# Attention and token-mixing kernel: head and token transposes moved from TensorE to transposing DMAs, with a new order of the mix steps and more products of zeros at the start

## The chip, the cores and the metric

The kernel runs on one core of one Trainium2 chip. The metric is the device time of one execution in microseconds (us). A profile's span is about 1.9 us shorter than the time of the same run. All runs compared here are of the state "fast"; two timed runs that were marked slow (346.0 us in e8, 346.2 us in e12) are left out of ratios and medians. Ratios are computed as the mean time of one kernel's fast runs over that of the other's of the same rounds, so they are not quite the ratio of the medians that are quoted.

## The reference

Block-sparse attention (4 batches, 8 heads, 768 tokens, 64 per head), then a residual MLP that first mixes tokens, then channels:

```python
scores = scale * np.matmul(q, k.transpose(0, 1, 3, 2))
mask = (abs(blk_i - blk_j) <= 1) | first and last blocks | sampled blocks
attn = softmax(np.where(mask, scores, -1e9))
x = (attn @ v), heads side by side            # (4, 768, 512)
a1 = alpha1 * x + beta1
u = x + lam * np.einsum('ts,bsd->btd', w_tok, a1)
a2 = alpha2 * u + beta2
out = u + lam * (np.maximum(a2 @ w_ch1, 0.0) @ w_ch2)
```

## The kernel before

A head pair is worked off in nine **units**. A unit is 1,024 score columns in PSUM and one exponential on ScalarE; there are 16 pairs, so 144 units. The products of attention and values follow two units later. When a pair is done, its **token mix** is queued, and between the units a filler emits first-layer (ch1) and second-layer (ch2) products.

The scores need q and k with the head dimension on partitions, so each head is transposed. Rows 64 to 87 of the transposed tiles hold the mask as 24 more contraction rows (block indicators in `kx`, mask values in `qx`), loaded once:

```python
def prepare(b, n):
    q2, k2, v2 = loaded.pop((b, n))
    rel = wk.tile([P, 2, NT, 2 * D], BF, name="rel", tag="rel", bufs=2)
    for i, src in enumerate((q2, k2)):
        nc.vector.tensor_copy(out=rel[:, :, :, i * D : (i + 1) * D], in_=...)
    yield
    for a in range(2):
        flat = transposes(rel, a)          # six TensorE transposes into an "mm" tile
        h = (2 * n + a) % NQB
        nc.vector.tensor_copy(out=qx[h][0:D, :], in_=flat[0:D, :])
        nc.vector.tensor_copy(out=kx[h][0:D, :], in_=flat[D:P, :])
        yield
# pair_mix(b, n), its end: the mixed tokens transposed for the first layer
    up = mm_tile([P, NT, P], BF)
    for t in range(NT):
        nc.tensor.transpose(up[:, t, :], ub[:, t, :], identb[:])
    nc.vector.tensor_copy(out=uTs[b][:, n, :], in_=up[:]...)
# mix_next(i): when a queued mix may start its VectorE part
    if m["dry"] and m["due"] <= i and (i >= len(units) or 1 <= i % NU <= 4):
```

The `mm` tiles (two PSUM buffers) serve these transposes, the token mix and the first layer alike. Cuts are marked with "..." or left out between functions.

The softmax here doesn't subtract the row's maximum and nothing guards it: scores larger than these inputs give would overflow.

Of the kernel before, what the change touches and what calls it, by code (L numbers as in the profile page):

```python
# [13 lines left out]
BF = mybir.dt.bfloat16  # L14
I32 = mybir.dt.int32
# [21 lines left out]
NS = NPAIR * NU  # L37
LAG = 2
SCALE = 1.0 / 8.0
EXPB = -0.35667494  # L40
# [23 lines left out]
def kernel(  # L64
# [33 lines left out]
    ).astype(np.float32)  # L98
    kbi_np = np.tile(np.arange(NBLK, dtype=np.float32), (NBLK, 1))

    tab_np = np.concatenate([mstat_np, kbi_np], axis=1)

    ident_dr = nc.inline_tensor(ident_np, name="ident_c")
    ind_dr = nc.inline_tensor(ind_np, name="ind_c")
    tab_dr = nc.inline_tensor(tab_np, name="tab_c")

# [18 lines left out]
    identb = pp.tile([P, P], BF, name="identb", tag="identb")  # L125
    qx = [pp.tile([P, S], BF, name=f"qx{i}", tag=f"qx{i}") for i in range(NQB)]
    kx = [pp.tile([P, S], BF, name=f"kx{i}", tag=f"kx{i}") for i in range(NQB)]
    vext = [
# [23 lines left out]
    q2f = wk.tile([P, 2, NT * D], FP, name="q2f", tag="hts", bufs=2)  # L152
    k2f = wk.tile([P, 2, NT * D], FP, name="k2f", tag="hts", bufs=2)
    nc.sync.dma_start(q2f[:, 0, :], pair_ap(q, 0, 0)[:, 0, :])
    nc.scalar.dma_start(k2f[:, 0, :], pair_ap(k, 0, 0)[:, 0, :])
    nc.sync.dma_start(sampi[MB, :], sampled_blocks.bitcast(I32))
    nc.scalar.dma_start(tab[MB, :], tab_dr.ap())
    nc.sync.dma_start(identb[:], ident_dr.ap())
    nc.scalar.dma_start(kx[0][MB, :], ind_dr.ap())
    nc.sync.dma_start(q2f[:, 1, :], pair_ap(q, 0, 0)[:, 1, :])  # L160
    nc.sync.dma_start(k2f[:, 1, :], pair_ap(k, 0, 0)[:, 1, :])
    for i in range(1, NQB):
        nc.sync.dma_start(kx[i][MB, :], ind_dr.ap())

    def load_pair(b, n):
# [20 lines left out]

    keep_warm(7, 512)
    for t in vext:
        nc.vector.memset(t[:, :, :, D:VW], 1.0)


# [18 lines left out]

    rel0 = wk.tile([P, 2, NT, 2 * D], BF, name="rel", tag="rel", bufs=2)

# [8 lines left out]

    def transposes(rel, a, slots=range(NT)):
        tps = mm_tile([P, NT, P], BF)
        for o in slots:
            nc.tensor.transpose(tps[:, o, :], rel[:, a, o, :], identb[:])  # L225
        return tps[:].rearrange("p o c -> p (o c)")

    first_cast(0)
    bq_ps = ps.tile([P, UN], FP, name="sps", tag="sps", bufs=2)
    for w in (0, 1):  # L230
        nc.tensor.matmul(
            bq_ps[0:NBLK, w * 512 : w * 512 + HS],
            mbb[MB, :],
            kx[0][MB, ts(w, HS)],
            start=True,
            stop=True,
        )
    flatA = transposes(rel0, 0, range(0, 3))
    flatB = transposes(rel0, 0, range(3, 6))
    nc.vector.tensor_copy(out=qx[0][MB, 0:HS], in_=bq_ps[0:NBLK, 0:HS])  # L240
    nc.scalar.copy(out=qx[0][MB, HS:S], in_=bq_ps[0:NBLK, 512 : 512 + HS])
    nc.vector.tensor_copy(out=kx[0][0:D, 0:HS], in_=flatA[D:P, 0:HS])
# [4 lines left out]
    for j in range(1, NQB):  # L247
        nc.sync.dma_start(qx[j][MB, :], qx[0][MB, :])


    def prepare(b, n):

        q2, k2, v2 = loaded.pop((b, n))
        vs[(b, n)] = v2
        rel = wk.tile([P, 2, NT, 2 * D], BF, name="rel", tag="rel", bufs=2)
        for i, src in enumerate((q2, k2)):
            nc.vector.tensor_copy(  # L257
                out=rel[:, :, :, i * D : (i + 1) * D],
                in_=src[:].rearrange("p h (o d) -> p h o d", o=NT),
            )  # L260
        yield
        for a in range(2):
            flat = transposes(rel, a)
            h = (2 * n + a) % NQB
            nc.vector.tensor_copy(out=qx[h][0:D, :], in_=flat[0:D, :])  # L265
            nc.vector.tensor_copy(out=kx[h][0:D, :], in_=flat[D:P, :])  # L266
            yield

    vs = {}
# [69 lines left out]
    def pair_mix(b, n):  # L339
# [19 lines left out]
        for g in range(NT // m):  # L359
            tp = mm_tile([P, m, P])  # L360
            for j in range(m):
                for s in range(NT):
                    nc.tensor.matmul(  # L363
                        tp[:, j, :],
                        wtokT[:, s, ts(m * g + j, P)],
                        a1p[:, s, :],
                        start=(s == 0),
                        stop=(s == NT - 1),
                    )
                if m == 2 and j == 0:  # L370
                    yield NT * T_MM128, 1, True
            gs = slice(m * g, m * g + m)
            sl = x_sb[:, s0 + m * g : s0 + m * g + m, cs]
            nc.vector.tensor_tensor(out=sl, in0=sl, in1=tp[:], op=ALU.add)  # L374
            nc.vector.tensor_tensor(  # L375
                out=ub[:, gs, :], in0=sl, in1=bc(a2_bc, m), op=ALU.mult
            )
            wait = 1 if g < NT // m - 1 else 5 if last else 2
            yield (1 if m == 2 else m) * NT * T_MM128, wait
        up = mm_tile([P, NT, P], BF)  # L380
        for t in range(NT):
# [9 lines left out]
    def ch1_group(k, f, tail):  # L391
# [8 lines left out]
        for dk in range(4):  # L400
# [6 lines left out]
            )  # L407
        if f % 2 == 0:
            nc.scalar.activation(  # L409
                hts[k][:, f, :], hp[:, 0:HS], AF.Relu, bias=b1t[:, f : f + 1], scale=1.0  # L410
            )
        else:
            nc.vector.tensor_scalar(  # L413
                out=hts[k][:, f, :],
                in0=hp[:, 0:HS],
                scalar1=b1t[:, f : f + 1],
                scalar2=0.0,
                op0=ALU.add,
                op1=ALU.max,
            )  # L420
# [36 lines left out]

    def setup_ch():
        nc.vector.tensor_copy(out=be2b[:], in_=be2T[:])
        for g in range(4):  # L460
            bp = mm_tile([P, 4])
            for f in range(4):
                for dk in range(4):
                    nc.tensor.matmul(
                        bp[:, f : f + 1],
                        w1b[:, dk, ts(4 * g + f, P)],
                        be2b[:, dk : dk + 1],
                        start=(dk == 0),
                        stop=(dk == 3),
                    )  # L470
            nc.vector.tensor_copy(out=b1t[:, ts(g, 4)], in_=bp[:])
            yield 16 * 30, 1

# [16 lines left out]
    for g in range(3):  # L490
        nc.gpsimd.dma_start(
            wtk[:, 2 * g : 2 * g + 2, :], wtk_ap[:, 2 * g : 2 * g + 2, :]
        )
    for t, src in ((lam_bc, moe_lam), (a1_bc, moe_alpha1), (b1_bc, moe_beta1)):
        nc.gpsimd.dma_start(t[:], src.unsqueeze(0).to_broadcast([P, DM]))
    loaded[(0, 2)] = load_pair(0, 2)
    loaded[(0, 3)] = load_pair(0, 3)
# [18 lines left out]
    def ch_next(tail=False):  # L516
# [4 lines left out]
        can1 = (  # L521
            g1 < NF1 and k1 // 2 < st["mixed"] and (k1 < 2 or g2 >= 12 * (k1 - 1))
        )
        can2 = g2 < NF2 and (
            g1 > 16 * (k2 + 1) or g1 == 16 * (k2 + 1) and st["at"] < st["i"]
# [18 lines left out]
    def mix_next(i):  # L544

        for m in mixq[:3]:
            if m["dry"] and m["due"] <= i and (i >= len(units) or 1 <= i % NU <= 4):
                m["due"] = i + next(m["gen"])[1]
# [27 lines left out]
    for i in range(len(units) + LAG):  # L576
# [3 lines left out]
        if i < len(units):  # L580
            b, n, u = units[i]
            pi = b * NPAIR + n
            emit_qk(b, n, u)
            if i == 2:

                vs[(0, 0)] = loaded.pop((0, 0))[0]
                put_v(0, 0)
                first_cast(1)
                flat = transposes(rel0, 1)
                nc.vector.tensor_copy(out=qx[1][0:D, :], in_=flat[0:D, :])  # L590
                nc.vector.tensor_copy(out=kx[1][0:D, :], in_=flat[D:P, :])
            if u == 0:
                if 0 < pi and pi + 3 < len(pairs):
# [4 lines left out]
            if i in (20, 22, 24, 26):  # L598
# [6 lines left out]
                )  # L605
            if u == 5 and pi + 1 < len(pairs):
                prep = prepare(*pairs[pi + 1])
            if prep is not None and u in (5, 7, 0):
                next(prep, None)
            if u == 8 and pi + 1 < len(pairs):  # L610
                put_v(*pairs[pi + 1])
            if i == 8:
                mix_add(None, setup_tok(), i)
            if i == 11:
                nc.vector.tensor_mul(out=a1_bc[:], in0=a1_bc[:], in1=lam_bc[:])
                nc.vector.tensor_mul(out=b1_bc[:], in0=b1_bc[:], in1=lam_bc[:])
            if i == NS:
                mix_add(None, setup_ch(), i)
            if NS + 10 <= i < NS + 26 and i % 2 == 0:
# [17 lines left out]
        if i >= LAG:  # L637
# [5 lines left out]
            while pv_done < lim:  # L643
# [3 lines left out]
                if r == GP - 1:  # L647
                    mix_add(pairs[j], pair_mix(*pairs[j]), max(i, 12))
        if mixq and not (i < NS and i % NU in (7, 0)):
            spent += mix_next(i)  # L650
# [42 lines left out]
```

## Time and profile before

| | before |
|---|---|
| median of 3 runs | 353.97 us (352.94 to 357.5) |
| span of the profiled run | 355.1 us |
| granted clock, mean over the span | 0.979 |
| exponentials number 1, 37, 55 and 144 start at | 8.9, 50.1, 89.5, 286.1 us |

In the views PE is TensorE, PEld its weight loads, DVE VectorE, ACT ScalarE, POOL GpSimd and SPq the queue of SyncE, from which the transposing DMAs are issued in order. The granted clock is the share of full speed that TensorE's clock was given.

The four exponentials cut the span into batch 0 (units 0 to 35), a stretch in which the later work is being filled in (units 36 to 53), and a regular rest. The views that carry the argument are printed in the prediction. The profiled run of before is one of its slower ones: its device time was 357.0 us. A difference of spans against it therefore overstates the gain by some 2 us, and I use medians for totals.

### The profile page before, as it was taken

What the parts mean: (1) busy time and instruction counts of PE and PEld (TensorE: products, weight loads), DVE (VectorE), ACT (ScalarE), POOL (GpSimd) and SP (SyncE); (2) the same over time, 40 slices, a digit from 0 to 9 for tenths busy, and PEclk for the clock granted to TensorE, in tenths of its full rate; (3) what the DMA queues carried; (4) which work ended last, traced back from release to release, by engine and by line L of the source; (5) the groups of instructions that cost most, each with busy time, mean ns of one, the idle gap of its engine ahead of it and who ended that gap; (6) DMA issues with size and microseconds to landing.
All of it is one profiled execution on the core that took longest, in us unless ns stands there. A gap on an engine that the chain in (4) does not pass through costs nothing.

```text
span 355.1 us, 7814 instructions
## 1 busy us (share of the span) xinstructions
PE 333.2 (94%) x3375; PEld 220.2 (62%) x3410; DVE 210.8 (59%) x416; ACT 193.7 (55%) x213; POOL 43.4 (12%) x67
## 2 busy tenths in 40 slices
PE   7989998989899999999999999999999999999995
PEld 3578776765575666566666667566666656555542
DVE  3399996576785665665674755665674655242321
ACT  3898996545756656556556646566656630212110
POOL 4666334010010101002010000000000000000000
PEclk9999997789999999999999999999999999999999
DMA  5999999503132240603242000000000000001012
GB/s 132 203 220 224 207 207 201 86 3 45 22 41 30 49 78 2 99 30 50 50 54 44 31 32 0 31 31 0 31 32 0 31 31 30 31 30 61 30 40 79
DMA packets 20518, 23.34 MB, mean 66 GB/s; under 512 B 1756, under 2 KB 16260, under 8 KB 20484
## 3 DMA queue, kind: packets, MB, share of 16 engines
q0 software_dynamic: 15984, 15.47, 27.4%
q1 hardware_dynamic: 4284, 7.14, 5.6%
q8 instruction: 26, 0.43, 0.5%
q10 hardware_dynamic: 216, 0.24, 0.2%
q14 instruction: 8, 0.07, 0.1%
HBM read 30.86 MB, written 6.29 MB: 105 GB/s over the span
## 4 chain that ended last, share of the span: by engine, by line
PE 78%; DVE 15%; ACT 3%; issue 2%; DMA 1%; ACTq 0%; DVEq 0%
PE cp L433 20%; PE mm L401 19%; PE sps L290 14%; PE mm L363 8%; PE ops L311 7%; PE sps L401 3%; PE ops L433 3%; PE mm L225 2%; DVE x_sb L328 2%; ACT eT L299 2%; DVE a1p L350 2%; DVE a1p L353 1%; DVE kx L266 1%; DVE ub L375 1%; DVE x_sb L374 1%
## 5 line engine op out<-in xcount | busy, mean ns | idle before, releaser
L299 ACT ACTIVATE eT<-sps,expb 128x1024 f16<-128x1024 f32 x144 | 157.5, 1114 | 91.4 <-PE sps L290 91.3
L290 PE MATMUL sps<-qx,kx 88*128 88x512 bf16 (+1 forms) x384 | 91.0, 341 | 1.7 <-DVE kx L266 0.9
L401 PE MATMUL mm<-uT,w1b 128*128 128x384 bf16 x436 | 87.6, 325 | 4.7 <-DVE uT L383 3.3
L433 PE MATMUL cp<-w2b,hts 128*128 128x512 bf16 x303 | 78.6, 379 | 2.5 <-DVE ot L442 0.8
L401 PEld LDWEIGHTS <-w1b 128*128 128x128 bf16 x512 | 48.2, 97 | 38.9 <-issue 4.8
L311 PEld LDWEIGHTS <-eT 128*128 128x128 f16 x1152 | 56.0, 100 | 24.5 <-DVE x_sb L328 1.9
L409 ACT ACTIVATE hts<-mm,b1t 128x384 bf16<-128x384 f32 x64 | 37.0, 578 | 50.7 <-PE mm L401 50.0
L433 PEld LDWEIGHTS <-hts 128*128 128x128 bf16 x384 | 36.2, 97 | 34.2 <-issue 1.0
L311 PE MATMUL ops<-vext,eT 128*128 128x65 f16 x1008 | 53.8, 197 | 0.9 <-DVE x_sb L328 0.8
L290 PEld LDWEIGHTS <-kx 88*128 88x128 bf16 x384 | 32.4, 101 | 15.5 <-issue 2.7
L363 PE MATMUL mm<-a1p,wtokT 128*128 128x128 bf16 x576 | 41.2, 225 | 0.8 <-ACT hts L409 0.8
L363 PEld LDWEIGHTS <-wtokT 128*128 128x128 bf16 x576 | 34.8, 101 | 1.4 <-issue 0.9
L413 DVE TENSOR_SCALAR hts<-mm,b1t 128x384 bf16<-128x384 f32 x45 | 27.7, 616 | 9.1 <-PE mm L401 8.5
L374 DVE TENSOR_TENSOR x_sb<-x_sb,mm 128x384 f32<-128x384 f32 (+1 forms) x35 | 18.1, 518 | 24.3 <-PE mm L363 24.0
L265 DVE COPY qx<-mm 64x768 bf16<-64x768 bf16 x30 | 16.4, 547 | 26.2 <-PE mm L225 26.1
L442 DVE TENSOR_TENSOR ot<-x_sb,cp 128x512 f32<-128x512 f32 x21 | 14.4, 685 | 18.6 <-PE cp L433 18.6
L413 DVE TENSOR_SCALAR hts<-sps,b1t 128x384 bf16<-128x384 f32 x19 | 11.7, 617 | 20.2 <-PE sps L401 20.2
L171 POOL DMA_DIRECT2D q<-in_q_dram x15 | 10.7, 712 | 90.5 <-DVE rel L257 83.5
L325 DVE RECIPROCAL rcp<-ops 128x6 f32<-128x6 f32 x28 | 5.4, 193 | 23.2 <-PE ops L311 23.2
L375 DVE TENSOR_TENSOR ub<-x_sb,a_bc 128x384 bf16<-128x384 f32 (+1 forms) x35 | 18.3, 524 | 1.2
L225 PEld LDWEIGHTS <-rel 128*128 128x128 bf16 x192 | 14.4, 103 | 6.4 <-issue 2.9
L225 PE MATMUL mm<-identb,rel 128*128 128x128 bf16 x192 | 17.3, 230 | 0.6 <-ACT hts L409 0.6
(64 smaller groups left out, 210.4 us busy)
## 6 DMA issues: line engine op xcount, KB each, us to landing
out_dram<-ot SPq DMA_DIRECT2D x24, 256.0 KB, 2.0
v<-in_v_dram POOLq DMA_DIRECT2D x16, 192.0 KB, 5.2
q<-in_q_dram POOLq DMA_DIRECT2D x15, 192.0 KB, 6.0
k<-in_k_dram POOLq DMA_DIRECT2D x15, 192.0 KB, 6.2
w1b<-in_moe_w_ch_dram POOLq DMA_DIRECT2D x4, 512.0 KB, 10.4
w2b<-in_moe_w_ch_dram POOLq DMA_DIRECT2D x4, 512.0 KB, 15.6
wtk<-in_moe_w_tok_dram POOLq DMA_DIRECT2D x3, 384.0 KB, 8.0
a_bc<-in_moe_alpha_dram POOLq DMA_DIRECT2D x2, 256.0 KB, 8.8
```

What stands on the lines that cost most here:

```text
L225: nc.tensor.transpose(tps[:, o, :], rel[:, a, o, :], identb[:])
L265: nc.vector.tensor_copy(out=qx[h][0:D, :], in_=flat[0:D, :])
L290: nc.tensor.matmul(sps[:, f - u * UN : f - u * UN + w], kx[h][0:KC, ts(jt, P)], qx[h][0:KC, c : c + w], start=True, stop=True,)
L299: nc.scalar.activation(eT[:], sps[:], AF.Exp, bias=expb[:], scale=SCALE)
L311: nc.tensor.matmul(ops[(b, n, a)][:, t * VW : t * VW + D + 1], eTs[(b, n, u)][:, ts(c, P)], vx[:, a, jt, 0 : D + 1], start=(r == 0), stop= ...
L363: nc.tensor.matmul(tp[:, j, :], wtokT[:, s, ts(m * g + j, P)], a1p[:, s, :], start=(s == 0), stop=(s == NT - 1),)
L374: nc.vector.tensor_tensor(out=sl, in0=sl, in1=tp[:], op=ALU.add)
L375: nc.vector.tensor_tensor(out=ub[:, gs, :], in0=sl, in1=bc(a2_bc, m), op=ALU.mult)
L401: nc.tensor.matmul(hp[:, 0:HS], w1b[:, dk, ts(f, P)], uTs[b][:, dk, ts(hf, HS)], start=(dk == 0), stop=(dk == 3),)
L409: nc.scalar.activation(hts[k][:, f, :], hp[:, 0:HS], AF.Relu, bias=b1t[:, f : f + 1], scale=1.0)
L413: nc.vector.tensor_scalar(out=hts[k][:, f, :], in0=hp[:, 0:HS], scalar1=b1t[:, f : f + 1], scalar2=0.0, op0=ALU.add, op1=ALU.max,)
L433: nc.tensor.matmul(cps[k][:], hts[k][:, nk, ts(m, P)], w2b[:, nk, :], start=(nk == 0), stop=(nk == 15),)
```

## The change

The intent is to take transposes off TensorE. From the eighth pair on, q and k with their mask columns are laid out as 128-column blocks in SBUF, and one transposing DMA each writes the whole of `qx` and `kx` of the pair. The mixed tokens of batches 1 to 3 (but for the last pair) go the same way. The rest is order: a mix may start in any unit, first and second layer start later, beta2 is folded in over several units, loads are reordered, the relus after the last unit go to ScalarE alone, and more products of zeros run on TensorE during the first loads.

```diff
+DMA_FROM = 7
+def mask_columns():
+    bt = mm_tile([P, NT, NBLK])
+    for o in range(NT):
+        nc.tensor.matmul(bt[:, o, :], kx[0][MB, ts(o, P)], mbb[MB, :], start=True, stop=True)
+    for i in (1, 0):
+        for j, src in enumerate((bt, indt)):
+            for a in range(2):
+                nc.vector.tensor_copy(out=rel[i][j][:, a * NT : (a + 1) * NT, D:KC], in_=src[:])
+def prepare_dma(b, n):
+    q2, k2, vs[(b, n)] = loaded.pop((b, n))
+    for j, (src, dst) in enumerate(((q2, qx2[i]), (k2, kx2[i]))):
+        nc.vector.tensor_copy(out=rel[i][j][:, :, 0:D]..., in_=src[:]...)
+        nc.sync.dma_start_transpose(dst[:]..., rel[i][j][:]...)
 # pair_mix
+        if b > 0 and not last:
+            nc.sync.dma_start_transpose(uTs[b][:, n, :]..., ub[:]...)
+            yield 0, 3
+            return
 # order
-            if m["dry"] and m["due"] <= i and (i >= len(units) or 1 <= i % NU <= 4):
+            if m["dry"] and m["due"] <= i:
-            g1 < NF1 and k1 // 2 < st["mixed"] and (k1 < 2 or g2 >= 12 * (k1 - 1))
+            g1 < NF1 and k1 // 2 < st["mixed"] and st["i"] > NS + 10 and (k1 < 2 or g2 >= 12 * (k1 - 1))
-        can2 = g2 < NF2 and (
+        can2 = st["i"] > NS + 24 and g2 < NF2 and (
 # zeros
-    keep_warm(7, 512)
+    keep_warm(6, 512)
+    keep_warm(2, 512)          # after the mask product
+    keep_warm(1, P)
+            if 1 <= i <= 4:
+                keep_warm(1, 512)
+            if i == NS + 3:
+                mask_columns()
```

## The prediction

> **What bounds the kernel now.** I read the page from the top: busy shares, then the slices, then the windows of 10 us, then the timeline where a window looked wrong, then the groups.
>
> The page of the kernel before, busy shares and slices (busy tenths; PEclk is the granted clock in tenths):
> ```profile
> PE 333.2 (94%) x3375; PEld 220.2 (62%) x3410; DVE 210.8 (59%) x416; ACT 193.7 (55%) x213; POOL 43.4 (12%) x67
> PE   7989998989899999999999999999999999999995
> PEclk9999997789999999999999999999999999999999
> ```
> TensorE is the busy engine, but matmul ends are modelled, so 94% proves nothing. I check it by start-to-start times in the timeline, in steady state (columns: start, duration, instructions):
> ```profile
> 180.97 0.81 PE L401 MATMUL mm<-uT,w1b 128*128 128x384 bf16 x4
> 181.62 1.03 PE L433 MATMUL cp<-w2b,hts 128*128 128x512 bf16 x4
> 182.48 0.28 PE L311 MATMUL ops<-vext,eT 128*128 128x65 f16 x4
> 182.60 0.50 PE L382 MATMUL mm<-identb,ub 128*128 128x128 bf16 x6
> 182.94 0.60 PE L290 MATMUL sps<-qx,kx 88*128 88x512 bf16 x2
> 183.37 0.50 PE L225 MATMUL mm<-identb,rel 128*128 128x128 bf16 x6
> 184.59 0.81 PE L401 MATMUL mm<-uT,w1b 128*128 128x384 bf16 x4 [0.72 <-DVE uT L383]
> ```
> Differences of starts: four first-layer products take 0.65 us, four second-layer products 0.86, a score unit (1,024 columns) 0.43, six transposes 0.34, eight attention-value products 0.24; further on, 18 token-mix products take 1.01. A head pair is 9 units, so TensorE needs 9 x 0.43 + 9 x 0.24 + 2 x 1.01 + 3 x 0.34 + 8 x 0.65 + 6 x 0.86 = 19.4 us. The exponentials that open units 18 apart start at 201.62 and 241.93 us, so a pair really takes 20.16 us. From about 85 us on, TensorE is therefore the bound to within 4%, and after the last exponential (286 us) it is busy 9.9 of every 10 us. Part of the 4% is the wait in the last line: a transpose result sits in one of the two shared PSUM buffers until VectorE copies it out, and the next product waits.
>
> The early part is different. Windows (us; PE, PEld, DVE, ACT, POOL busy; granted clock; DMA):
> ```profile
> 30.00:40.00 10.00, 9.65 (x154) 7.76 (x154) 9.61 (x23) 9.89 (x10) 4.19 (x6) 1.00 1.10 215
> 50.00:60.00 10.00, 8.64 (x140) 6.67 (x138) 7.74 (x19) 7.50 (x7) 4.28 (x6) 0.86 1.28 203
> 60.00:70.00 10.00, 9.65 (x128) 8.17 (x126) 5.18 (x13) 4.71 (x5) 0.71 (x1) 0.63 0.78 119
> 70.00:80.00 10.00, 7.74 (x90) 6.17 (x91) 7.75 (x14) 4.66 (x5) 1.43 (x2) 0.83 0.04 3
> 230.00:240.00 10.00, 9.95 (x108) 6.80 (x108) 6.41 (x12) 5.42 (x6) 0.00 (x0) 1.00 0.08 28
> ```
> In batch 0 (9 to 50 us) ScalarE and VectorE are full. At 54 to 80 us TensorE starves behind VectorE (1.4 us for the cast of beta2, 1.8 us for ub), its clock falls to half at 57 to 67.5 and 74 to 78 us, and 14 units take 26 us.
>
> **What the skill says.** "TensorE: Matmul & The Clock Gate", Part 1, gives half rate after an idle window of about 3.4 us and a 56 ns spacing of warm 128-column products. The trace agrees on size: 0.34/6 = 56 ns; and the same score unit lasts 1.04 us at 12 us and 0.60 us at 20 us. It differs in one thing: the clock column says 1.00 at 10 to 16 us, but eight attention-value products last 0.64 us there and 0.41 us after 18 us, so the array was at half rate until about 16 us whatever the column says. "Advanced Engine Details and Errata", X-Bar Transpose (TRN2), says transposing DMAs are as fast as regular ones, and that two transpose streams must not be in flight together; "DMA: Bandwidth & Descriptors", Latency and other measured facts, gives 261 GB/s for one transposing kernel. No transposing DMA is in this trace; its plain 256 KB output lands in 2.0 us. All new transposes are issued from one queue (SyncE), so the corruption case doesn't arise.
>
> **The change part by part.** *1. Head transposes.* Pairs 8 to 16 (counted from one: nine pairs) lose 12 TensorE transposes each, 108 in all, at 56 ns = 6.1 us. VectorE loses four copies per pair, 36 x 0.55 = 20 us:
> ```profile
> L265 DVE COPY qx<-mm 64x768 bf16<-64x768 bf16 x30 | 16.4, 547 | 26.2 <-PE mm L225 26.1
> L266 DVE COPY kx<-mm 64x768 bf16<-64x768 bf16 x30 | 16.8, 559 | 0.4
> L383 DVE COPY uT<-mm 128x768 bf16<-128x768 bf16 x16 | 8.8, 551 | 2.6 <-PE mm L382 2.5
> ```
> In their place stand two DMAs of 128 x 1,536 bf16 (393 KB) per pair. At the skill's 261 GB/s that is 1.5 us each, by estimate 2 x 1.5 + 2 = 5 us for both. They are issued in unit 1 of the pair before and needed in unit 0 of the next: 8 x 2.24 = 18 us of room. The casts before them stay as they were (two of 0.36 us).
> *2. Mixed tokens.* 11 of 16 groups lose six transposes (66 x 56 ns = 3.7 us) and one VectorE copy (11 x 0.55 = 6 us). The DMA of 197 KB has three units, about 6 us.
> Both lie where TensorE is the bound, so the 174 x 56 ns = **9.7 us** come off the end. The waits that these results caused on TensorE at 80 to 290 us are 3.3 us for uT and 1.0 us for kx by the view of waits; I count on **3 us** of them, since some will pass to the next user of the two buffers.
> *3. Mask columns.* Six small products (0.2 us) and eight VectorE copies of 144 columns, about 0.2 us each by the 193 ns of the small reciprocal: 1.6 us on VectorE at unit 39, in the starved stretch, **+0.5 us**. The GpSimd memsets run before 5 us, where that engine waits for the mask anyway.
> *4. Products of zeros.* Six instead of seven at first, then two and a short one, then four of 512 columns (0.22 us each warm, 0.43 cold). They fill gaps at 6 to 11 us. If the clock comes up one window (3.4 us) earlier, units 3 to 5, 0.3 us slow each, and the 0.8 us gap before unit 3 shrink; if not, the four cost up to 0.9 us. **-1 us**.
> *5. Order in batch 0.* TensorE waits 1.15 us at 25 us for a copy behind VectorE's table products; they now come two units later, and the loads are reordered. **-1 us**.
> *6. Units 36 to 54.* By counting the instructions of both orders with the durations above, TensorE has 27.5 us of work in these 18 units before and 28.7 after; the trace took about 50.1 to 85.8 us, 35.7. So 8 us were lost to idling and half clock. After the change a token mix may start in any unit, the beta2 products are spread over five units, and the first layer waits until unit 47. VectorE stays nearly full here, so I count on half: **-4 us**.
> *7. The tail.* Relus go to ScalarE alone: 0.578 us per 0.65 + 0.86 us of TensorE work, so not on the path. **0**.
> Sum: -9.7 - 3 + 0.5 - 1 - 1 - 4 = **-18.2 us**; 353.97 - 18.2 = 336. A second way agrees: all TensorE work at the warm rates is 316 us before and 308 after. After: 9 us of start, 40 for batch 0, 31.5 for units 36 to 54, then 242 us of work with 5% on top = 254, and 2 for the last output: 336 us in the profile.
>
> **The rivals.** *The transposes come late.* For it: nothing here has measured one, and they share one in-order queue with the outputs, each waiting for VectorE. Against it: 18 us of room for some 5. If a 393 KB transpose took over 9 us, each of nine pairs would wait some microseconds: 345 to 365 us. I give this 6%. *Another engine takes the bound.* In the steady windows VectorE is at 6.4 and ScalarE at 5.5 of 10, and VectorE gets 26 us less; so no, except in batch 0 and units 36 to 54. *The early stretch does not mend.* VectorE gets the mask copies exactly where it is full, and a stall of 1.4 us was enough to lose the clock before. Then parts 4 to 6 give nothing, and the time is 353.97 - 12 = 342 us; I give this a good quarter. *The opposite:* the clock never falls, all 8 us of part 6 and 3 us at the start come back: 329 us.
>
> **Range and chances.** The middle is 336 us; 328 to 344 us covers an early stretch that mends fully or not at all. Faster by over 2% means under 346.9 us: part 1 and 2 alone give 344.3, so only late transposes or a new stall spoil it.
>
> **What would show it.** Right: transposes left at 84 for heads, 30 for mixed tokens; a steady pair of about 19.0 us instead of 20.16; no score product waiting for a DMA; transposing DMAs landing in 2 to 6 us; granted clock above 0.9 at 50 to 80 us; the last exponential near 270 us. Wrong: score or first-layer products waiting for a transposing DMA; a pair still at 20 us, with the saved time turned into waits for the two PSUM buffers; the clock at half again around 55 to 70 us.

## The result, and the profile after

The changed kernel took 340.93 us (median of 4 runs, 340.88 to 343.96), the kernel before 355.24 us in the same rounds; the ratio is 0.9618 (95%: 0.953 to 0.971). The prediction was 336 us with a range of 328 to 344, so it was right, with 5 us of the forecast 18 missing.

The page of the changed kernel:

```profile
PE 322.6 (95%) x3248; PEld 205.9 (61%) x3248; DVE 177.9 (52%) x360; ACT 203.6 (60%) x230; POOL 45.3 (13%) x71
PE   7998988689989999999999999999999999999995
PEclk9999999999999999999999999999999999999999
```

VectorE (DVE) lost 33 us of work and TensorE looks as busy as before, which is what a bound engine looks like when it is given less to do: the span shrinks with it. In the regular part nothing of TensorE's stream is a transpose any more (timeline, columns: start, duration):

```profile
194.31 0.28 PE L359 MATMUL ops<-vext,eT 128*128 128x65 f16 x4
194.43 1.03 PE L488 MATMUL cp<-w2b,hts 128*128 128x512 bf16 x4
195.29 0.60 PE L338 MATMUL sps<-qx,kx 88*128 88x512 bf16 x2
195.73 0.81 PE L456 MATMUL mm<-uT,w1b 128*128 128x384 bf16 x4
196.47 1.02 PE L488 MATMUL cp<-w2b,hts 128*128 128x512 bf16 x4
```

The transposing DMAs (operation, count, median us from issue to landing):

```profile
uT<-ub SPq DMA_TRANSPOSE x11, 2.8
qx<-rel1q SPq DMA_TRANSPOSE x5, 3.9
kx<-rel1k SPq DMA_TRANSPOSE x5, 4.0
qx<-rel0q SPq DMA_TRANSPOSE x4, 3.8
kx<-rel0k SPq DMA_TRANSPOSE x4, 5.1
```

The trace shows the landing of only seven of the 29, 2.8 to 5.1 us after the issue began (in e9 heads took up to 8 us at 90 to 130 us), with some 18 us of room, and the view of waits has no score or first-layer product that waits for one. The windows that answer to those shown before:

```profile
50.00:60.00 10.00, 8.62 (x125) 6.32 (x122) 9.45 (x26) 7.07 (x7) 2.48 (x4) 1.00 1.29 203
60.00:70.00 10.00, 6.99 (x138) 5.60 (x138) 6.37 (x16) 5.34 (x5) 1.58 (x3) 1.00 0.48 73
70.00:80.00 10.00, 9.11 (x119) 6.49 (x117) 7.69 (x15) 6.10 (x8) 0.74 (x2) 1.00 0.16 21
```

The clock stayed full in this execution, but TensorE still idles at 60 to 70 us. The exponentials say where the time went:

| | before | after | difference |
|---|---|---|---|
| exponential 1 starts | 8.93 us | 8.59 us | -0.3 |
| 1 to 37 (batch 0) | 41.20 us | 43.87 us | +2.7 |
| 37 to 55 | 39.41 us | 36.07 us | -3.3 |
| 55 to the end of the span | 265.5 us | 250.6 us | **-14.9** |

All of the gain lies after the 55th exponential. The part before it, where I had expected 5.5 us, gained 1.0 us, and that with a clock at half rate for 13.6 us in the one trace and for none in the other. Of the forecast's signs, 84 and 30 transposes are left on TensorE, and the last exponential starts at 275.6 us, not near 270.

### The profile page after: what moved, and what is told of

Read it like the earlier page. It is cut to its first block, busy times and chain, and to the rows that moved or that the text cites. A ratio compares the mean times of both kernels' runs of the same rounds, so it can differ in the third digit from the quotient of the medians.

```text
span 339.1 us, 7582 instructions
## 1 busy us (share of the span) xinstructions
PE 322.6 (95%) x3248; PEld 205.9 (61%) x3248; DVE 177.9 (52%) x360; ACT 203.6 (60%) x230; POOL 45.3 (13%) x71
## 3 DMA queue, kind: packets, MB, share of 16 engines
q1 hardware_dynamic: 41344, 16.42, 23.2%
## 4 chain that ended last, share of the span: by engine, by line
PE 80%; DVE 12%; ACT 4%; issue 2%; DMA 1%; SPq 0%; ACTq 0%
PE cp L488 21%; PE mm L456 19%; PE sps L338 14%; PE mm L411 8%; PE ops L359 8%; ACT eT L347 3%; PE sps L456 3%; PE ops L488 3%; DVE x_sb L376 2%; DVE a1p L398 1%; PE mm L243 1%; DVE kx L299 1%; DVE qx L298 1%; DVE ot L497 1%; DVE x_sb L422 1%
## 5 line engine op out<-in xcount | busy, mean ns | idle before, releaser
L347 ACT ACTIVATE eT<-sps,expb 128x1024 f16<-128x1024 f32 x144 | 157.4, 1114 | 77.1 <-PE sps L338 76.5
L338 PE MATMUL sps<-qx,kx 88*128 88x512 bf16 (+1 forms) x384 | 87.6, 330 | 0.3
L488 PE MATMUL cp<-w2b,hts 128*128 128x512 bf16 x336 | 84.5, 378 | 1.1 <-DVE ot L497 1.0
L359 PEld LDWEIGHTS <-eT 128*128 128x128 f16 x1152 | 53.5, 98 | 26.8 <-DVE x_sb L376 5.2
L411 PE MATMUL mm<-a1p,wtokT 128*128 128x128 bf16 x576 | 39.3, 219 | 1.2 <-DVE kx L299 0.9
L411 PEld LDWEIGHTS <-wtokT 128*128 128x128 bf16 x576 | 33.0, 98 | 2.3 <-DVE kx L299 1.1
L186 POOL DMA_DIRECT2D v<-in_v_dram x16 | 11.6, 724 | 84.3 <-DVE vext L322 71.0
L376 DVE TENSOR_TENSOR x_sb<-ops,rcp 128x384 f32<-128x384 f32 x28 | 15.6, 557 | 1.0
L401 DVE TENSOR_TENSOR a1p<-a1p,b_bc 128x768 bf16<-128x768 bf16 x16 | 15.3, 958 | 0.6
L398 DVE TENSOR_TENSOR a1p<-x_sb,a_bc 128x768 bf16<-128x768 f32 x16 | 15.3, 957 | 0.5
L464 ACT ACTIVATE hts<-sps,b1t 128x384 bf16<-128x384 f32 x17 | 9.9, 581 | 9.1 <-PE sps L456 8.6
```

The costliest lines, as they stand in the source:

```text
L186: nc.gpsimd.dma_start(t[:], pair_ap(src, b, n))
L338: nc.tensor.matmul(sps[:, f - u * UN : f - u * UN + w], kx[h][0:KC, ts(jt, P)], qx[h][0:KC, c : c + w], start=True, stop=True,)
L347: nc.scalar.activation(eT[:], sps[:], AF.Exp, bias=expb[:], scale=SCALE)
L359: nc.tensor.matmul(ops[(b, n, a)][:, t * VW : t * VW + D + 1], eTs[(b, n, u)][:, ts(c, P)], vx[:, a, jt, 0 : D + 1], start=(r == 0), stop= ...
L376: nc.vector.tensor_tensor(out=x_sb[:, s0 : s0 + NT, h * D : (h + 1) * D], in0=op[:, :, 0:D], in1=rcp[:].unsqueeze(2).broadcast_to([P, NT, D]),
L398: nc.vector.tensor_tensor(out=a1p[:], in0=x_sb[:, s0 : s0 + NT, cs], in1=bc(a1_bc, NT), op=ALU.mult)
```

## The experiments

Two theories stood at first. **A:** the gain is TensorE time and the waits for the `mm` buffers in the regular part. **B:** it is mostly the new order and the zeros. Later, of the early part: **V:** VectorE's queue sets its time; **C:** only the clock does; and, for transposes issued earlier, **D:** they meet the weight loads.

All results in one table. "To 55" is the start of the 55th exponential in the profiled run, "rest" the span after it, "half" the us at half clock before it by the trace's clock records (counted from the clock's first rise).

| run | median us | ratio to before | to 55 | rest | half |
|---|---|---|---|---|---|
| before | 353.97 | 1 | 89.5 | 265.5 | 13.6 |
| changed kernel | 340.93 | 0.9618 | 88.5 | 250.6 | 0 |
| e1 DMA only | 346.15 | 0.9761 | 90.8 | 253.2 | 13.6 |
| e2 order only | 356.81 | 1.0072 | 90.9 | 264.2 | 6.8 |
| e3 heads only | 346.22 | 0.9756 | 92.9 | 252.6 | 13.6 |
| e4 old mix rule | 342.40 | 0.9647 | 89.3 | 251.8 | 3.4 |
| e5 mask on GpSimd | 342.00 | 0.9624 | 88.0 | 250.6 | 0 |
| e6 from pair 6 | 349.78 | 0.9843 | 98.1 | 250.0 | 20.5 |
| e7 from pair 4 | 366.07 | 1.0292 | 113.3 | 249.7 | 34.1 |
| e8 old zeros | 342.14 | 0.9615 | 87.0 | 250.6 | 0 |
| e9 from pair 7 | 340.48 | 0.9556 | 88.7 | 250.1 | 6.8 |
| e10 relief | 355.98 | 1.0018 | 105.2 | 250.6 | 23.8 |
| e11 relief, from pair 7 | 353.48 | 0.9954 | 102.2 | 250.2 | 17.0 |
| e12 changed again | 342.55 | 0.9615 | 91.3 | 250.6 | 10.2 |

The column "rest" is the first lesson: for one instruction order it repeats to 0.1 us (250.6 in e5, e8, e10, e12 and the changed kernel), so it can be compared from single profiles. What differs from run to run is the early part, and there the clock.

**e1: the DMA transposes alone.** The kernel before, with `mask_columns`, `prepare_dma` and the two `dma_start_transpose` calls grafted in, old order and old zeros.

```diff
+            if i == NS + 3:
+                mask_columns()
-            if u == 5 and pi + 1 < len(pairs):
+            if u == 5 and pi + 1 < min(len(pairs), DMA_FROM):
                 prep = prepare(*pairs[pi + 1])
+            if u == 1 and DMA_FROM <= pi + 1 < len(pairs):
+                next(prepare_dma(*pairs[pi + 1]))
```

> The kernel before with nothing but the DMA transposes (heads of the last nine pairs, mixed tokens of batches 1 to 3, the mask columns). Theory A, the gain is TensorE time: 174 transposes of 56 ns = 9.7 us, some 3 us of waits on the two shared PSUM buffers, less 1.3 us of mask copies: about 11 us under the kernel before, ratio 0.965 to 0.975, and 0 to 4 us over the changed kernel. Rival B, most of the gain is the new order and the zero products: under 6 us, ratio over 0.98.

Measured: 346.15 us, ratio 0.976, between the two theories' numbers and close to A. It lies 5.2 us over the changed kernel, where A had at most 4. The rest shrank by 12.3 us, as A has it, and the early part grew by 1.3 us with the clock at half for exactly as long as before (13.6 us).

**e2: the order and the zeros alone.** (Left out of the edit, here and in e3: the pause before the mixed tokens' transposes is two units again.)

```diff
-DMA_FROM = 7
+DMA_FROM = 99
-            if i == NS + 3:
-                mask_columns()
-        if b > 0 and not last:
+        if False:
```

> The changed kernel with every transpose back on TensorE and without mask columns, so the new order and zero products alone. Theory A: 0 to 4 us under the kernel before, ratio 0.99 to 1.0. Rival B: 8 us or more under it, ratio under 0.98. If both parts help each other (the freed VectorE time is what makes the early stretch pass), this run plus the one with DMA transposes alone gain less together than the change does.

Measured: 356.81 us, ratio 1.007. B falls: the order alone gains nothing. But the two parts are not simply added: -8.7 us (e1) and +2.0 us (e2) against the medians of before of that call, 354.84, make -6.7, and the change makes -14. With the same order, the DMA transposes are worth 356.8 - 340.9 = 16 us; with the old order, 8.7. Of the rest, 13.6 us and 12.3 us: there the difference is small. The remaining interaction lies in the early part, where the runs also had different clocks, so I do not divide it further. All four runs of e1 had a clock of 0.970 to 0.980, those of the changed kernel 0.980 to 0.998: beside the DMA transposes the new order may save falls of the clock, which no run here separates from the rest of it.

**e3: heads by DMA, mixed tokens on TensorE.**

```diff
-        if b > 0 and not last:
+        if False:
```

> The changed kernel with the mixed tokens back on TensorE in all batches; heads stay with the DMA. Theory A: 66 x 56 ns = 3.7 us more, and up to 3 us of waits for the PSUM buffers come back: 344.5 to 348 us, ratio to the kernel before 0.97 to 0.98. If waits and not TensorE time make the gain, the copy of 0.55 us on VectorE shows as a wait before the first-layer products of over 3 us in all; if the mixed tokens are worth nothing, it stays at 341.

Measured: 346.22 us, in the expected range, but by the wrong way. The rest is only 2.0 us longer than in the changed kernel, though by counting instructions it has 3.4 us more of TensorE work; the other 3 us came from an early part with 13.6 us at half clock. So the mixed tokens are worth 2 us in the regular part, less than their 56 ns each. (Its one run at a clock of 0.995 took 344.35 us, 3.4 us more than the changed kernel's at that clock; one run is too little to set against the repeating part.)

**e4: the old rule for starting a mix.**

```diff
-            if m["dry"] and m["due"] <= i:
+            if m["dry"] and m["due"] <= i and (i >= len(units) or 1 <= i % NU <= 4):
-        if mixq:
+        if mixq and not (i < NS and i % NU in (7, 0)):
```

> The changed kernel with the old rule of when a token mix may start (units 1 to 4 of a pair) and step. The changed trace shows batch 0 longer by 2.7 us (43.9 against 41.2 us from the first exponential to the 37th). Theory A: the free rule puts the mix's VectorE work in front of the next pair's copies; with the old rule the 37th exponential starts near 50 us again, and the end moves by -2 to +1 us, since VectorE's work is only put off to the next units. Rival: the lost time is the rule's and the end comes 2.5 us or more earlier, or the new rule is what mends the units after and the end comes over 3 us later.

Measured: 342.40 us, no difference that the noise would let pass. The 37th exponential started at 49.3 us instead of 52.5, and the 18 units after it took 40.0 us instead of 36.1: what the free rule costs in batch 0 it has done of the next stretch's work. My expectation of the 37th was right. The end came 1.5 us later by the medians, a little over the expected 1 us but within the scatter of the runs.

**e5: mask copies on GpSimd.**

```diff
+        nc.vector.tensor_copy(out=bts[:], in_=bt[:])
-            for j, src in enumerate((bt, indt)):
+            for j, src in enumerate((bts, indt)):
-                    nc.vector.tensor_copy(
+                    nc.gpsimd.tensor_copy(
```

> The changed kernel with seven of the eight mask copies given to GpSimd: VectorE does one copy from PSUM (about 0.25 us) instead of eight that took 1.6 us in the trace at 57.3 to 58.6 us. Theory V, in units 36 to 54 VectorE's queue sets the time: the 55th exponential comes about 1 us earlier and the end 0.5 to 2 us earlier (338.5 to 340.5 us). Rival C, the loss there is the clock alone: no change within 0.5 us unless the clock falls in the one and not in the other.

Measured: 342.00 us in the median (340.4 to 343.9); in two profiles without a fall of the clock the 55th exponential came 0.5 us earlier (88.0 against 88.5) and the rest is equal to 0.1 us. The stretch from exponential 37 to 55 took 35.6 us, against 36.1 in the changed kernel and in e8. So the mask copies cost some 0.5 us, as the prediction said; V's 1 us was too much, and the end that V expected, 338.5 to 340.5 us, was missed.

**e6 and e7: transposes from the sixth and from the fourth pair on,** mask on GpSimd, and the mixed tokens of batch 0 too; the cast in unit 4 for these early pairs, so that VectorE does not wait for the loads.

```diff
-DMA_FROM = 7
+DMA_FROM = 5                  # e7: 3
-            if i == NS + 3:
+            if i == 16:       # e7: 10
-                elif pi + 1 >= DMA_FROM and u == 1:
+                elif pi + 1 >= DMA_FROM and u == (1 if pi > 5 else 4):
-        if b > 0 and not last:
+        if not last:
```

> As the run with mask copies on GpSimd, with DMA transposes two pairs earlier (from the sixth pair) and for the mixed tokens of batch 0 as well. It takes 8 copies of 0.55 us for heads and 4 for mixed tokens off VectorE before unit 63, 6.6 us in all, and 48 TensorE transposes (2.7 us). Theory V: the 55th exponential 3 to 5 us earlier than in the changed kernel, the end at 334 to 337.5 us. Rival D, the transposes meet the weight loads (16 DMA engines full until 66 us) and come late: score or first-layer products wait for a DMA by more than 1 us each, and the end is at 340 us or later.

> The same from the fourth pair on, so also the last pair of batch 0 and the first of batch 1: another 4.4 us off VectorE and 1.3 us off TensorE. Theory V: 1 to 3 us under the run from the sixth pair. Rival D: equal or slower than that, with a wait for a transposing DMA at units 27 or 36 when the loads are densest.

Measured: 349.78 and 366.07 us. D holds, by more than I had expected. In the run from the sixth pair the SyncE queue shows the third issue of mixed tokens and the first two of heads (start, us the issue took):

```profile
53.98 1.21 SPq L431 DMA_TRANSPOSE uT<-ub  x1
57.04 4.84 SPq L313 DMA_TRANSPOSE qx<-rel1q  x1
61.98 8.27 SPq L313 DMA_TRANSPOSE kx<-rel1k  x1
```

and the same two in the changed kernel, when the loads are over:

```profile
91.09 1.44 SPq L311 DMA_TRANSPOSE qx<-rel1q  x1
92.70 1.91 SPq L311 DMA_TRANSPOSE kx<-rel1k  x1
```

While the loads keep the DMA engines full (share 1.2 to 1.3 in the windows from 50 to 65 us), the issue of a head transpose itself takes 4.8 and 8.3 us; the 18 of the changed kernel take 1.4 to 3.9. The first three issues of mixed tokens, half as large, took only 1.2 to 1.6 us, but the first of them landed 10.9 us after it began. The `kx` transpose lands 13.2 us after its issue began, and TensorE stands still:

```profile
75.18 1.04 PE L340 MATMUL sps<-qx,kx 88*128 88x512 bf16 x3 [10.64 <-DMA kx<-rel1k]
```

After ten idle microseconds the clock is at half as well: that product, 0.60 us in the steady part, takes 1.04. In the run from the fourth pair one such wait was 22.5 us. Begun among the loads, the transposes cost more than they save; for the seventh pair, whose transposes start at 71.6 us, e9 shows no such loss.

**e8: the old zeros.**

```diff
-    keep_warm(6, 512)
+    keep_warm(7, 512)
-    keep_warm(2, 512)
-    keep_warm(1, P)
-            if 1 <= i <= 4:
-                keep_warm(1, 512)
```

> The changed kernel with the zero products of before (seven of 512 columns at the start, none later). If the products are worth something, the clock comes up later than 13.8 us and the tenth exponential starts 0.5 to 1.5 us later, the end 0.5 to 1.5 us later. If they are worth nothing[...], the end is within 0.5 us of the changed kernel.

Measured: 342.14 us in the median, ratio 0.9615, the same as with the zeros. The profiled run, in which the clock happened to come up at 6.3 us, was the fastest of that kernel (339.4 us). Over all profiles here the first rise lies anywhere from 3.9 to 16.3 us, with and without the zeros. No gain of the zeros can be seen; the runs are too few to exclude one of a microsecond.

**e9: heads from the seventh pair on,** mask on GpSimd as in e5.

```diff
-DMA_FROM = 7
+DMA_FROM = 6
```

> The changed kernel with mask copies on GpSimd and heads by DMA from the seventh pair instead of the eighth. In the changed trace the loads end at 66 us; this pair's transposes are issued in unit 46, near 70 us, so they meet empty DMA engines, unlike those from the sixth pair (issued at 57 us, 8.3 us to issue, 10.6 us of wait). It takes 4 copies of 0.55 us off VectorE and 12 transposes (0.7 us) off TensorE in units 45 to 54. Theory D (only the loads make them late): no score product waits for a DMA, the end 1 to 2.5 us earlier than the changed kernel of the same rounds. If the transposes are late for another reason, the wait shows again at unit 54 and the end is no earlier.

Measured: 340.48 us against 342.55 of the changed kernel on the same chip (e12), ratios to before 0.9556 and 0.9615: 2.1 us less, as expected of D, and no product waits for a DMA, though the first transpose, beside loads of later pairs, landed only 9.9 us after its issue began. The two runs at clock 1.00 took 338.1 and 338.3 us. This is the fastest version measured; that it beats the changed kernel is likely but not shown, since the difference is small beside the spread of their runs (338.1 to 342.5 and 340.9 to 343.6).

**e10 and e11: work taken off VectorE,** e11 with e9's edit too.

```diff
 def scale_w2(g, w2b):
-        nc.vector.tensor_tensor(
+        nc.gpsimd.tensor_tensor(
 # prepare_pe, pairs 6 and 7 only; and uT copies of batch 0 from unit 36 on
-            nc.vector.tensor_copy(out=kx[h][0:D, :], in_=flat[D:P, :])
+                nc.scalar.copy(out=kx[h][0:D, :], in_=flat[D:P, :])
```

> The changed kernel with work taken off VectorE in units 36 to 62 and none off TensorE: mask copies and the eight scalings of the second weights (0.68 us each) to GpSimd, four kx copies and two mixed-token copies (0.55 us each) to ScalarE, some 10 us of VectorE time. Theory V: the 55th exponential 3 to 5 us earlier, the end 2.5 to 5 us earlier. Rival: TensorE's own work (28.7 us in those units) and the clock set the time there, or GpSimd slows VectorE by as much: under 1 us.

> Both of these together. If they act on the same wait they gain less together than apart; theory V: 335 to 338.5 us where the changed kernel takes 341 to 342.

Measured: 355.98 and 353.48 us, as slow as before. The experiment failed for a reason of its own. Timeline of VectorE, then of GpSimd, in e10:

```profile
83.21 10.38 DVE L292 COPY relp<-q 128x768 bf16<-128x768 bf16 x1
93.51 0.35 DVE L292 COPY relp<-k 128x768 bf16<-128x768 bf16 x1
```

```profile
73.09 9.78 POOL L536 TENSOR_TENSOR w2b<-w2b,lam_bcb 128x1024 bf16<-128x1024 bf16 x4 [9.59 <-DVE lam_bcb L535]
85.02 8.35 POOL L536 TENSOR_TENSOR w2b<-w2b,lam_bcb 128x1024 bf16<-128x1024 bf16 x4
```

A VectorE copy that takes 0.35 us in the median lasted 10.38 us, until the four GpSimd multiplications beside it (2.3 us each, 0.68 on VectorE) were over at 93.4 us; TensorE waited 9.6 us for the relu behind it. The Trainium skill, "Advanced Engine Details and Errata", Miscellaneous Facts, GPSIMD Details, says that GpSimd shares a read and a write interface with VectorE and that the two conflict in some forms; the trace agrees, and adds that a copy can be held back through four GpSimd instructions in a row. In e11 the same happened to a VectorE multiplication (9.43 us). So these two runs say nothing of theory V.

**e12: the changed kernel again.** The file is unchanged but for a comment.

> The changed kernel once more, to compare the three others with it on one chip, and to see how time and granted clock go together over more runs: 340.9 to 344 us, the slower ones at a clock of 0.98.

Measured: 342.55 us in the median; single runs at a clock of 0.998, 0.989 and 0.985 took 340.9, 342.6 and 343.6 us. Its profile has 10.2 us at half clock, a 55th exponential at 91.3 instead of 88.5 us, and the same rest. What goes before a fall of the clock can be read from windows of one clock period: within one trace the changes of the clock lie multiples of 3.41 us apart (before: 16.25, 57.21, 67.45, 74.28, 77.69 us), and this grid begins elsewhere in each run. Kernel before, then the changed kernel, then e12, e3 and e4 (columns as before: TensorE's busy time follows the length of the window, and the granted clock is the last but two):

```profile
53.80:57.20 3.40, 2.04 (x43) 1.56 (x41) 2.70 (x8) 1.92 (x3) 1.35 (x2) 1.00 1.30 201
57.20:60.60 3.40, 3.40 (x40) 2.44 (x37) 1.58 (x5) 2.46 (x3) 2.14 (x3) 0.50 1.32 202
```

```profile
58.20:61.60 3.40, 2.14 (x42) 1.65 (x39) 2.80 (x10) 2.23 (x2) 1.43 (x2) 1.00 1.28 193
61.60:65.00 3.40, 2.78 (x49) 2.14 (x45) 2.02 (x5) 1.41 (x2) 0.00 (x0) 1.00 0.83 128
```

```profile
62.80:66.20 3.40, 1.63 (x30) 1.13 (x29) 2.66 (x6) 2.12 (x2) 0.00 (x0) 1.00 0.43 67
```

```profile
53.22:56.64 3.42, 2.35 (x34) 1.48 (x32) 3.32 (x7) 2.49 (x3) 0.99 (x3) 1.00 1.31 201
56.64:60.05 3.41, 3.41 (x32) 2.82 (x29) 2.19 (x11) 1.11 (x1) 1.95 (x3) 0.50 1.31 202
```

```profile
51.31:54.73 3.42, 1.94 (x39) 1.51 (x36) 3.25 (x9) 2.24 (x3) 1.13 (x2) 1.00 1.29 206
54.73:58.14 3.41, 2.01 (x34) 1.28 (x32) 2.92 (x12) 2.23 (x2) 2.15 (x4) 1.00 1.31 198
```

At 2.04 of 3.40 us busy the clock fell, at 2.14 it did not, and e12's window of 1.63 cost it 10.2 us at half rate. But there is no sharp limit between: e3 lost the clock after 2.35 us, and e4 kept it after 1.94. Over the 14 traces, cut by their own periods, the clock fell after all 18 windows at full clock in which TensorE was busy for 1.65 us or less, and after none above 2.5 us; between 1.7 and 2.5 both occur. So a gap-rich window tends to lose the clock, and the same instructions, cut by the period at another place, keep or lose it; what decides between 1.7 and 2.5 us stays open.

## Why the prediction was right, and where it was off

*Parts 1 and 2, the transposes (-9.7 and -3 us): right.* The rest shrank by 14.9 us. By counting weight loads in the traces, 9.4 us of that are 168 transposes (the other six lay before the 55th exponential) and 2.4 us are 15 first-layer products of 0.16 us that the new order had already done by then; what is left, 3.1 us, I put down to waits. The pair's mean from unit 72 to 135 fell from 20.2 to 19.2 us; 19.0 was forecast. Within it, e3 shows that the mixed tokens gave 2.0 us, not 3.7: the heads brought more than their share, by the waits. From e2 to e3, where only the heads change, the rest shrank by 11.6 us, of which 108 transposes are 6.0; TensorE's waits behind the copies of `kx` at 90 to 276 us fell too (first e2, then e3; us in total, times, longest):

```profile
PE mm L437 <- DVE kx L299: 2.7, 6, 0.4
PE mm L456 <- DVE kx L299: 1.7, 3, 0.6
```

```profile
PE mm L456 <- DVE kx L299: 0.3, 1, 0.3
```

From e3 to the changed kernel the listed waits of TensorE in that stretch grew again, from 1.5 to 2.5 us, now for relus and output additions: a part of what the mixed tokens freed.

*Part 3, mask copies (+0.5 us): right,* by e5, though the copies took 0.3 us from PSUM and 0.19 from SBUF, 1.9 us in all and not 1.6.

*Part 4, zeros (-1 us): not seen* (e8).

*Part 5, order in batch 0 (-1 us): wrong in sign.* The stretch grew by 2.7 us, since mixes now start there; e4 shows that this is work done early. With the old mix rule (e4) the stretch took 40.6 us, 0.6 less than before, so the order without the free rule did go the way that was forecast.

*Part 6, units 36 to 54 (-4 us): the step that failed.* "VectorE stays nearly full here, so I count on half" took lost time for something that the change would mend. The reading under it was off as well: the 18 units took 39.4 us (50.13 to 89.54), not 35.7, so by the same count 11.9 us were lost and not 8; and 11 exponentials, not 14, start between 54 and 80 us. In the two traces TensorE idles 4.8 us there before (39.41 minus 34.57 busy) and 5.4 us after (36.07 minus 30.70), with 1.2 us more work after. The 3.3 us by which the stretch shrank go with the clock of those executions: in e12, the same kernel with the clock at half for 10.2 us, the stretch took 39.3 us. Nor is VectorE full: it is busy 26.3 of 39.4 us before and 27.9 of 36.1 after. Moving single pieces of its work gave 0.5 us (e5) or was drowned (e10), so whether its queue or the to and fro between TensorE and VectorE sets the pace stays open. What the record does show is rarer falls of the clock: its mean is 0.992 over the nine fast runs of the changed kernel and 0.984 over the 44 of before in the rounds of the experiments. Their medians (341.7 and 355.1 us) differ by 13.4 us and their fastest runs (340.88 and 352.78) by 11.9, near the 12.2 of parts 1 to 3, so by estimate the clock is worth some 1.5 us of the gain and little else came of the early part.

*Part 7, relus in the tail (0): right* as far as it shows; TensorE is busy 10.0 of every 10 us from 280 us to the last products.

*The rivals.* Late transposes did not happen, but only because the change begins after the loads: e6 and e7 are that rival, at 349.8 and 366.1 us. "The early stretch does not mend", 342 us with a good quarter of the chance, is what came, and the sign named for it, the clock at half around 55 to 70 us, is there in e12 (66.2 to 76.5 us). The range held because it was laid to take in this case, not because parts 4 to 6 came true. That is the weak point of the forecast: the middle should have been laid at 342, for the clock's falls differ from one execution to the next, and I counted those of a single, slower one as the kernel's own.

*The second way.* Its 336 us are a span, which would be 338 us of device time, so the two ways agreed less well than it says. They met by luck, too: it put the 55th exponential at 80.5 us (88.5 came) and the rest at 256 us (250.6 came).

## What to carry to other kernels

Where TensorE is the bound, a transpose moved to a DMA is worth its time on TensorE plus the wait for the PSUM buffer that it filled, provided that it is issued when the loads are over; issued among them it held TensorE for 10.6 us (e6) and 22.5 us (e7) at a time. Compare kernels by stages: the part that repeats to 0.1 us tells small gains from one profile, while a stretch in which the clock may fall needs many runs. A free engine is not free for any work: try GpSimd beside VectorE on one operation before moving several.

## What the Trainium skill lacked or had wrong

- "Advanced Engine Details and Errata", X-Bar Transpose (TRN2): transposing DMAs "are as fast as regular DMAs". Here 29 of them moved 9.2 MB (18 of 393 KB, 11 of 197 KB) and raised the hardware queue's packet time from 5.6% of 355 us to 23.2% of 339 us, so by my estimate, in which time beside other packets counts in full, about 59 us of the 16 engines, 157 GB/s; the plain transfers of that queue before moved 7.14 MB in 19.9 us, 359 GB/s. Packets under 512 B rose from 1,756 to 38,924.
- The same page and "DMA: Bandwidth & Descriptors" do not say how long the issue of a transposing DMA takes while other transfers fill the engines: 4.8 and 8.3 us for 393 KB here (e6), in which the queue issues nothing else, against 1.4 to 3.9 us when the loads are over.
- "TensorE: Matmul & The Clock Gate", Part 1, ties the fall of the clock to an idle window and does not say how much work a window may hold and still count as idle. Here it fell after windows in which TensorE was busy for 0 to 2.46 of 3.41 us, always up to 1.65, and was kept after some from 1.74 us on.
- No page says that a VectorE instruction can be held through several GpSimd instructions in a row: a 0.35 us copy lasted 10.38 us beside four GpSimd multiplications (e10), and a multiplication 9.43 us (e11).
